# An adaLN attention-and-MLP block rebuilt around small array tiles, exps shared by two engines, and tails fed into the attention loop

## The chip, the cores and the metric

One core of a Trainium2 chip. The metric is the device time of one execution in microseconds (us), the median of several. A ratio is the mean time of one kernel's fast runs over that of the kernel before in the same rounds, so it is not quite the ratio of the medians quoted. An experiment marked "one look" has a single run, whose state (fast or slow) is therefore unknown; runs of one kernel in rounds lay within 0.5% of each other.

## The reference

A transformer block of 2048 tokens, width 512, 32 heads of 16, MLP width 1376. Six modulation vectors come from one conditioning vector.

```python
h = layernorm(x) * (1 + ca) + sa
x = x + ga * (softmax(q @ k.T * 16**-0.5) @ v) @ wo     # q, k, v = h @ wqkv, 32 heads of 16
h = layernorm(x) * (1 + cb) + sb
x = x + gb * (gelu(h @ w1 + b1) @ w2 + b2)
```

With a head width of 16, scores are small in contraction and values small in output, while the number of exps is large: 32 x 2048 x 2048.

## The kernel before

Everything is kept feature-major. Scores use the full contraction of 128 with a q tile in which all heads but one are masked to zero. Each value matmul writes 48 rows: 16 values, padding, 16 ones-columns for the denominator. Score groups of three and two tiles alternate, each with one PSUM buffer.

```python
def emit_qk(grp):                                   # grp: 3 or 2 pairs (head, key tile)
    for i, (g, kt) in enumerate(grp):
        nc.tensor.matmul(out=st[:, i, 0:qw], lhsT=kT[:, cch, kt * P:(kt + 1) * P],
                         rhs=qm[g][:, 0:qw], start=True, stop=True)
...
nc.scalar.activation(out=pt[:, 0:n, 0:qw], in_=st[:, 0:n, 0:qw], func=ACT.Exp, scale=0.25)
...
nc.tensor.matmul(out=od_cur[0:VM, 0:qw], lhsT=VE[:, kt, g % 4, :], rhs=pt[:, i, 0:qw],
                 start=(kt == 0), stop=(kt == NTT - 1))       # VM = 48
...
for bi, (q0, qw) in enumerate(blocks):              # 4 query blocks of 512
    attention(q0, qw, OTp)
    wo_and_residual(q0, qw, OTp)
    if bi < len(blocks) - 1:
        tail(q0, qw)                                # layernorm, MLP, store of this block
```

The softmax here doesn't subtract the row's maximum and nothing guards it: scores larger than these inputs give would overflow.

Of the kernel before, what the change touches and what calls it, by code (L numbers as in the profile page):

```python
# [9 lines left out]
ACT = mybir.ActivationFunctionType  # L10
ALU = mybir.AluOpType
BF16 = mybir.dt.bfloat16
FP32 = mybir.dt.float32
I32 = mybir.dt.int32


@with_exitstack
def kernel(
# [15 lines left out]
    P = 128  # L34
# [4 lines left out]
    NTT = S // P  # L39
    NTQ = S // 512  # L40
    NFC = (F + P - 1) // P
    EPS = 1e-5
    GELU_K = math.sqrt(2.0 / math.pi)
    VM = 48

    def frows(fc):
        return min(P, F - fc * P)

    const = ctx.enter_context(tc.tile_pool(name="const", bufs=1))
    wpool = ctx.enter_context(tc.tile_pool(name="wpool", bufs=1))  # L50
    resid = ctx.enter_context(tc.tile_pool(name="resid", bufs=1))

    xT = resid.tile([P, NC, S], BF16, name="xT")
    for j in range(NC):
        nc.sync.dma_start_transpose(out=xT[:, j, :], in_=A_x[0][:, j * P:(j + 1) * P])  # L55
# [3 lines left out]
    ones_bf = const.tile([P, P], BF16, name="ones_bf")  # L59
    nc.vector.memset(ones_bf, 1.0)  # L60

    pidx = const.tile([P, 1], I32, name="pidx")
    nc.gpsimd.iota(pidx, pattern=[[0, 1]], base=0, channel_multiplier=1)
    ph = const.tile([P, 1], I32, name="ph")
    nc.vector.tensor_scalar(out=ph, in0=pidx, scalar1=4, scalar2=None, op0=ALU.arith_shift_right)
    ph_f = const.tile([P, 1], FP32, name="ph_f")
    nc.vector.tensor_copy(out=ph_f, in_=ph)
    maskh = const.tile([P, 8], FP32, name="maskh")
    for g in range(8):
        nc.vector.tensor_scalar(out=maskh[:, g:g + 1], in0=ph_f, scalar1=float(g), scalar2=None,  # L70
                                op0=ALU.is_equal)
    magic = const.tile([P, 512], I32, name="magic")
    nc.vector.memset(magic, 0x5F3759DF)

    last_rows = F - (NFC - 1) * P
    b1c_bf = const.tile([P, NFC], BF16, name="b1c_bf")
    nc.vector.memset(b1c_bf, 0.0)
    nc.sync.dma_start(out=b1c_bf[:, 0:NFC - 1],
                      in_=B_b1[0:(NFC - 1) * P].rearrange("(j p) -> p j", p=P))
    nc.sync.dma_start(out=b1c_bf[0:last_rows, NFC - 1:NFC],  # L80
                      in_=B_b1[(NFC - 1) * P:F].rearrange("(p o) -> p o", o=1))
    b1c = const.tile([P, NFC], FP32, name="b1c")
    nc.vector.tensor_copy(out=b1c, in_=b1c_bf)

    b2c_bf = const.tile([P, NC], BF16, name="b2c_bf")
    nc.sync.dma_start(out=b2c_bf, in_=B_b2.rearrange("(j p) -> p j", p=P))
    b2c = const.tile([P, NC], FP32, name="b2c")
    nc.vector.tensor_copy(out=b2c, in_=b2c_bf)

    cc_bf = const.tile([P, NC], BF16, name="cc_bf")  # L90
    nc.sync.dma_start(out=cc_bf, in_=c.rearrange("o (j p) -> p (o j)", p=P))
    cc = const.tile([P, NC], FP32, name="cc")
    nc.vector.tensor_copy(out=cc, in_=cc_bf)

    wqkv_ctx = ExitStack()
    wqkv_pool = wqkv_ctx.enter_context(tc.tile_pool(name="wqkv_pool", bufs=1))
    W_mod = wqkv_pool.tile([P, NC, 6 * D], BF16, name="W_mod")
    nc.sync.dma_start(out=W_mod, in_=w_mod.rearrange("(j p) n -> p j n", p=P))
    W_qkv = wqkv_pool.tile([P, NC, 3 * D], BF16, name="W_qkv")
    nc.sync.dma_start(out=W_qkv, in_=A_wqkv.rearrange("(j p) n -> p j n", p=P))  # L100
    W_o_pad = wpool.tile([P, 8, D], BF16, name="W_o_pad")
    nc.vector.memset(W_o_pad, 0.0)
    wo_view = A_wo.rearrange("(t jj d) f -> jj d t f", t=8, jj=4, d=16)
    for jj in range(4):
        nc.sync.dma_start(out=W_o_pad[32 * jj:32 * jj + 16, :, :], in_=wo_view[jj])
    W_1 = wpool.tile([P, NC, F], BF16, name="W_1")
    nc.sync.dma_start(out=W_1, in_=B_w1.rearrange("(j p) n -> p j n", p=P))
    W_2 = wpool.tile([P, NFC, D], BF16, name="W_2")
    nc.vector.memset(W_2[:, NFC - 1, :], 0.0)
    nc.sync.dma_start(out=W_2[:, 0:NFC - 1, :],  # L110
                        in_=B_w2[0:(NFC - 1) * P, :].rearrange("(j p) n -> p j n", p=P))
    last_rows = F - (NFC - 1) * P
    nc.sync.dma_start(out=W_2[0:last_rows, NFC - 1, :], in_=B_w2[(NFC - 1) * P:F, :])

    hT = resid.tile([P, NC, S], BF16, name="hT")
    qT = resid.tile([P, NC, S], BF16, name="qT")
    kT = resid.tile([P, NC, S], BF16, name="kT")
    vT = resid.tile([P, NTT, D], BF16, name="vT")

    pkp_ctx = ExitStack()  # L120
    pkp = pkp_ctx.enter_context(tc.tile_pool(name="pro_keep", bufs=4))
    pspA_ctx = ExitStack()
    ppsA = pspA_ctx.enter_context(tc.tile_pool(name="proA_ps", bufs=4, space=bass.MemoryType.PSUM))
    ptpA_ctx = ExitStack()
    ptpA = ptpA_ctx.enter_context(tc.tile_pool(name="proA_tmp", bufs=2))
    means = []
    rstds = []
    for tq in range(NTQ):
        q0 = tq * 512
        cs = slice(q0, q0 + 512)  # L130
        xsq = ptpA.tile([P, NC, 512], BF16, name="ln_xsq")
        nc.vector.tensor_tensor(out=xsq, in0=xT[:, :, cs], in1=xT[:, :, cs], op=ALU.mult)
        ps1 = ppsA.tile([P, 512], FP32, name="ln_ps")
        for j in range(NC):
            nc.tensor.matmul(out=ps1, lhsT=ones_bf, rhs=xT[:, j, cs],
                             start=(j == 0), stop=(j == NC - 1))
        mean = pkp.tile([P, 512], FP32, name="p_mean")
        nc.vector.tensor_scalar(out=mean, in0=ps1, scalar1=1.0 / D, scalar2=None, op0=ALU.mult)
        ps2 = ppsA.tile([P, 512], FP32, name="ln_ps")
        for j in range(NC):  # L140
            nc.tensor.matmul(out=ps2, lhsT=ones_bf, rhs=xsq[:, j, :],
                             start=(j == 0), stop=(j == NC - 1))
        rstd = pkp.tile([P, 512], FP32, name="p_rstd")
        nc.vector.tensor_tensor(out=rstd, in0=mean, in1=mean, op=ALU.mult)
        nc.vector.tensor_scalar(out=rstd, in0=rstd, scalar1=-EPS, scalar2=None, op0=ALU.add)
        nc.vector.scalar_tensor_tensor(out=rstd, in0=ps2, scalar=1.0 / D, in1=rstd,
                                       op0=ALU.mult, op1=ALU.subtract)
        nc.scalar.activation(out=rstd, in_=rstd, func=ACT.Sqrt)
        nc.vector.reciprocal(out=rstd, in_=rstd)  # L149
        means.append(mean)  # L150
        rstds.append(rstd)
    pspA_ctx.close()
    ptpA_ctx.close()

    def rsqrt_fp32(tp, dst, src, width):
        si = src.bitcast(I32)
        ti = tp.tile([P, width], I32, name="rs_ti")
        nc.vector.tensor_scalar(out=ti, in0=si, scalar1=1, scalar2=None, op0=ALU.logical_shift_right)
        nc.vector.tensor_tensor(out=ti, in0=magic[:, 0:width], in1=ti, op=ALU.subtract)
        r = ti.bitcast(FP32)  # L160
        u = tp.tile([P, width], FP32, name="rs_u")
        for it in range(2):
            nc.vector.tensor_tensor(out=u, in0=r, in1=r, op=ALU.mult)
            nc.vector.tensor_tensor(out=u, in0=u, in1=src, op=ALU.mult)
            nc.vector.tensor_scalar(out=u, in0=u, scalar1=-0.5, scalar2=1.5,
                                    op0=ALU.mult, op1=ALU.add)
            dsti = dst if it == 1 else r
            nc.vector.tensor_tensor(out=dsti, in0=r, in1=u, op=ALU.mult)
            r = dsti

    def layernorm_fmajor(src, dst, acol, scol, col0, width, alloc_ps, tp, use_act=False):
        cs = slice(col0, col0 + width)
        xsq = tp.tile([P, NC, width], BF16, name="ln_xsq")
        nc.vector.tensor_tensor(out=xsq, in0=src[:, :, cs], in1=src[:, :, cs], op=ALU.mult)
        ps1 = alloc_ps(width)
        for j in range(NC):
            nc.tensor.matmul(out=ps1, lhsT=ones_bf, rhs=src[:, j, cs],
                             start=(j == 0), stop=(j == NC - 1))
        mean = tp.tile([P, width], FP32, name="ln_mean")
        nc.vector.tensor_scalar(out=mean, in0=ps1, scalar1=1.0 / D, scalar2=None,  # L180
                                op0=ALU.mult)
        ps2 = alloc_ps(width)
        for j in range(NC):
            nc.tensor.matmul(out=ps2, lhsT=ones_bf, rhs=xsq[:, j, :],
                             start=(j == 0), stop=(j == NC - 1))
# [346 lines left out]
```

## Time and profile before

1329.8 us (median of 5, 1327.56 to 1330.2). The page and the working by stage stand in the prediction.

| stage, from the trace | us |
|---|---|
| until the first exp | 96.0 |
| attention with the three inner tails between its matmuls | 1156.8 |
| after the last exp | 76.5 |

With 1061 us for attention alone, the three inner tails cost about 96 us (an estimate: the difference), not 160. It agrees with their work on PE: 430 recorded matmuls that are not attention lie in the middle stage, at most 93 us at 0.216 us each.

The page's "PE 93%" is an average over stages, and pipelined matmuls overlap, so it is the distance between the starts of matmul groups that says how full PE is.

### The profile page before, as it was taken

The page shows a single profiled execution, that of the slowest core. Times are in us where ns is not written, and L with a number is a line of the kernel's source. Part 1 is how long each engine was busy: PE and PEld are TensorE (multiplying, and loading weights), DVE is VectorE, ACT ScalarE, POOL GpSimd, SP SyncE. Part 2 cuts the span into 40 slices and gives each one's busy share as a digit, 9 for nine tenths or more (in the row PEclk, how much of TensorE's full clock was granted, in tenths as well). Part 3 has the DMA queues.
Part 4 walks back from the last instruction along what each step waited for, and adds up shares of the span by engine and source line. Part 5 has one row for each costly group of instructions (what it writes and reads, how often), then busy time and mean ns, then how long its engine had stood idle before and what let it go on. Part 6 is the DMA issues. An engine that isn't in the chain of part 4 may idle for free.

```text
span 1329.3 us, 13099 instructions
## 1 busy us (share of the span) xinstructions
PE 1231.2 (93%) x4986; PEld 406.8 (31%) x5080; DVE 624.7 (47%) x989; ACT 1050.9 (79%) x962; POOL 139.6 (11%) x139
## 2 busy tenths in 40 slices
PE   3689999999999999999999999999999999999756
PEld 1332222222233332222233332222233332222224
DVE  6851333333368733232378743332377743332356
ACT  1468899898979868989878868989878878989634
POOL 0020101111121101010121101011111111110000
PEclk9799999999999999999999999999999999999868
DMA  9200000000000000000000000000000000000000
GB/s 230 77 1 0 0 1 0 1 1 0 1 0 1 1 17 0 1 1 0 1 0 0 1 16 0 1 0 0 1 0 1 1 16 0 1 0 1 0 0 17
DMA packets 16718, 13.09 MB, mean 10 GB/s; under 512 B 11184, under 2 KB 15120, under 8 KB 16656
## 3 DMA queue, kind: packets, MB, share of 16 engines
q1 hardware_dynamic: 16656, 12.26, 3.4%
q8 instruction: 39, 0.64, 0.2%
q14 instruction: 23, 0.19, 0.0%
HBM read 8.07 MB, written 2.10 MB: 8 GB/s over the span
## 4 chain that ended last, share of the span: by engine, by line
PE 87%; DVE 6%; ACT 4%; issue 2%; SPq 1%; DMA 0%; ACTq 0%; DVEq 0%
PE od L367 38%; PE stA L335 22%; PE stB L335 15%; ACT pt L345 3%; PE auxT L407 2%; PE auxT L460 2%; PE ps_proj L275 2%; PE auxT L432 2%; DVE p_rstd L149 1%; PE ps_proj L266 1%; ACT g_th L451 1%; SPq L55 1%; PE f_m L460 1%; DVE g_t L444 0%; DVE gT L453 0%
## 5 line engine op out<-in xcount | busy, mean ns | idle before, releaser
L345 ACT ACTIVATE pt<-stA 128x1536 bf16<-128x1536 f32 x416 | 603.6, 1451 | 161.3 <-PE stA L335 143.6
L367 PE MATMUL od<-pt,VE 128*48 128x512 bf16 x2048 | 577.2, 386 | 6.1 <-issue 0.4
L345 ACT ACTIVATE pt<-stB 128x1024 bf16<-128x1024 f32 x400 | 407.1, 1018 | 3.0 <-PE stB L335 2.2
L335 PE MATMUL stA<-qm,kT 128*128 128x512 bf16 x1188 | 338.8, 383 | 20.9 <-ACT pt L345 16.0
L367 PEld LDWEIGHTS <-VE 128*48 128x48 bf16 x2048 | 174.6, 101 | 412.1 <-issue 307.6
L335 PEld LDWEIGHTS <-kT 128*128 128x128 bf16 x2048 | 143.9, 97 | 333.6 <-issue 257.6
L375 DVE COPY OStg<-od 16x512 f32<-16x512 f32 x128 | 87.1, 680 | 322.0 <-PE od L367 320.5
L335 PE MATMUL stB<-qm,kT 128*128 128x512 bf16 x780 | 237.3, 384 | 0.0
L310 DVE TENSOR_SCALAR qm<-qT,maskh 128x512 bf16<-128x512 bf16 x128 | 47.9, 379 | 239.3 <-PE stA L335 183.5
L318 POOL MEMSET VE<- 128x2048 bf16 x32 | 57.8, 1810 | 854.5 <-PE od L367 838.5
L379 DVE RECIPROCAL DStg<-DStg 128x512 f32<-128x512 f32 x32 | 106.8, 3336 | 0.1
L376 DVE COPY DStg<-od 16x512 f32<-16x512 f32 x128 | 87.6, 684 | 2.6
L407 PE MATMUL auxT<-OTp,W_o_pad 128*128 128x512 bf16 x127 | 37.5, 426 | 8.3 <-DVE OTp L381 5.6
L453 DVE SCALAR_TENSOR_TENSOR gT<-g_th,g_y 128x512 bf16<-128x512 bf16 (+3 forms) x55 | 31.9, 582 | 27.2 <-ACT g_th L451 26.4
L451 ACT ACTIVATE g_th<-g_t 128x512 bf16<-128x512 bf16 (+3 forms) x55 | 29.8, 543 | 13.5 <-DVE g_t L448 13.1
L432 PE MATMUL auxT<-hT,W 128*128 128x512 bf16 (+1 forms) x126 | 34.7, 380 | 4.8 <-DVE g_y L440 4.6
L319 POOL MEMSET VE<- 128x1024 bf16 x32 | 34.5, 1080 | 1.7
L432 PEld LDWEIGHTS <-W 128*128 128x128 bf16 (+1 forms) x220 | 21.6, 104 | 38.0 <-issue 25.3
L460 PEld LDWEIGHTS <-W 128*128 128x128 bf16 (+1 forms) x220 | 22.6, 104 | 28.3 <-issue 11.0
L460 PE MATMUL auxT<-gT,W 128*128 128x512 bf16 (+1 forms) x132 | 31.0, 379 | 0.0
L275 PE MATMUL ps_proj<-hT,W_qkv 128*128 128x512 bf16 x128 | 28.3, 379 | 0.0
L363 POOL MEMSET OStg<- 128x512 f32 x32 | 16.8, 526 | 101.8 <-DVE OTp L381 101.8
(101 smaller groups left out, 497.7 us busy)
## 6 DMA issues: line engine op xcount, KB each, us to landing
W_mod<-in_w_mod_dram SPq DMA_DIRECT2D x1, 3072.0 KB, 10.8
out_dram<-stage SPq DMA_DIRECT2D x16, 128.0 KB, 1.7
W_qkv<-in_A_wqkv_dram SPq DMA_DIRECT2D x1, 1536.0 KB, 15.8
W<-in_B_w_dram SPq DMA_DIRECT2D x1, 1376.0 KB, 18.5
W<-in_B_w_dram SPq DMA_DIRECT2D x1, 1280.0 KB, 20.6
W_o_pad<-in_A_wo_dram SPq DMA_DIRECT2D x4, 128.0 KB, 17.3
W<-in_B_w_dram SPq DMA_DIRECT2D x1, 96.0 KB, 16.0
xT<-in_A_x_dram SPq DMA_TRANSPOSE x4, 5.5
```

Of the source, the lines that this page charges most:

```text
L275: nc.tensor.matmul(out=ps, lhsT=W_qkv[:, j, col0:col0 + P], rhs=hT[:, j, cs], start=(j == 0), stop=(j == NC - 1))
L310: nc.vector.tensor_scalar(out=t[:, 0:qw], in0=qT[:, cch, q0:q0 + qw], scalar1=maskh[:, g:g + 1], scalar2=None, op0=ALU.mult)
L318: nc.gpsimd.memset(VE[:, :, :, 16:VM], 0.0)
L335: nc.tensor.matmul(out=st[:, i, 0:qw], lhsT=kT[:, cch, kt * P:(kt + 1) * P], rhs=qm[g][:, 0:qw], start=True, stop=True)
L345: nc.scalar.activation(out=pt[:, 0:n, 0:qw], in_=st[:, 0:n, 0:qw], func=ACT.Exp, scale=0.25)
L367: nc.tensor.matmul(out=od_cur[0:VM, 0:qw], lhsT=VE[:, kt, g % 4, :], rhs=pt[:, i, 0:qw], start=(kt == 0), stop=(kt == NTT - 1))
L375: nc.vector.tensor_copy(out=OStg[rb:rb + 16, 0:qw], in_=od_cur[0:16, 0:qw])
L376: nc.vector.tensor_copy(out=DStg[rb:rb + 16, 0:qw], in_=od_cur[32:48, 0:qw])
L379: nc.vector.reciprocal(out=DStg[:, 0:qw], in_=DStg[:, 0:qw])
L407: nc.tensor.matmul(out=ps[:, 0:qw], lhsT=W_o_pad[:, t, cc * P:(cc + 1) * P], rhs=OTp[:, t, 0:qw], start=(t == 0), stop=(t == 7))
L432: nc.tensor.matmul(out=u[:rows, 0:hw], lhsT=W_1[:, j, fc * P:fc * P + rows], rhs=hT[:, j, hcs], start=(j == 0), stop=(j == NC - 1))
L460: nc.tensor.matmul(out=ps[:, 0:hw], lhsT=W_2[:rows, fc, dc * P:(dc + 1) * P], rhs=gT[:rows, fc, hs], start=(fc == 0), stop=(fc == NFC - 1))
```

## The change

Its intent is to make attention cheap on PE by using parts of the array beside each other, to take a quarter of the exps off ACT, and to put projections and MLP into the gaps. The kernel is written anew, so the diff is cut to its core; the loading of inputs and the normalisation, now token-major, are left out.

```diff
+    for g in range(2):                             # a pair of score tiles; rows 64-127 or 0-63
+        i = 2 * half + g
+        rows = slice(32 * i, 32 * i + 32)          # two heads in 32 rows; one is masked in q
+        nc.tensor.matmul(out=st[:, g, :], lhsT=kT[cc][kb][rows, ko * P:(ko + 1) * P],
+                         rhs=qm[(cc, b, par)][rows, :], start=True, stop=True)
...
+        if half == 1 and s % 2 == 1:               # every fourth piece: exp on DVE, by bits
+            nc.vector.tensor_scalar(out=pt[:, 2:4, :].bitcast(I16), in0=st, scalar1=EXB,
+                                    scalar2=None, op0=ALU.add)
+        else:
+            nc.scalar.activation(out=pt[:, 2 * half:2 * half + 2, :], in_=st,
+                                 func=ACT.Exp, scale=ESC)
...
+    for i in range(4):                             # four heads in four 32-column tiles
+        nc.tensor.matmul(out=od[32 * i:32 * i + 32, :], lhsT=VE[kt][:, 8 * cc + 2 * i + par, :],
+                         rhs=pt[:, i, :], start=(kt == 0), stop=(kt == NT - 1),
+                         tile_position=(0, 32 * i))
...
+    for s in range(NS):                            # 512 slots: query block, head group, key tile
+        emit_exp(s)
+        ...                                        # slots 1, 5, 9: block_in of blocks 1 to 3
+        emit_qk(2 * s + 3)
+        emit_qk(2 * s + 4)
+        if s > 0:
+            emit_pv(s - 1)
+        pop()                                      # one unit of other work, or one dummy matmul
...
-            attention(q0, qw, OTp)
-            wo_and_residual(q0, qw, OTp)
-            if bi < len(blocks) - 1:
-                tail(q0, qw)
```

There are three score buffers of two tiles, three exp-output buffers (`pt`), one output accumulator (`od`), and one PSUM bank (`ax`) for all other work inside the slots. The denominators go through DRAM to be spread over partitions.

## The prediction

> **What bounds the kernel now.** I read the page first: busy shares, the slices, the chain that ended last; then the timeline of one steady stretch of attention, because shares are averages over stages; then a table by stage.
>
> ```profile
> span 1329.3 us, 13099 instructions
> PE 1231.2 (93%) x4986; PEld 406.8 (31%) x5080; DVE 624.7 (47%) x989; ACT 1050.9 (79%) x962; POOL 139.6 (11%) x139
> ...
> PE   3689999999999999999999999999999999999756
> ...
> ACT  1468899898979868989878868989878878989634
> ...
> PE 87%; DVE 6%; ACT 4%; issue 2%; SPq 1%; DMA 0%; ACTq 0%; DVEq 0%
> PE od L367 38%; PE stA L335 22%; PE stB L335 15%; ACT pt L345 3%; PE auxT L407 2%; PE auxT L460 2%; PE ps_proj L275 2%; PE auxT L432 2%; DVE p_rstd L149 1%; PE ps_proj L266 1%; ACT g_th L451 1%; SPq L55 1%; PE f_m L460 1%; DVE g_t L444 0%; DVE gT L453 0%
> ...
> L345 ACT ACTIVATE pt<-stA 128x1536 bf16<-128x1536 f32 x416 | 603.6, 1451 | 161.3 <-PE stA L335 143.6
> L367 PE MATMUL od<-pt,VE 128*48 128x512 bf16 x2048 | 577.2, 386 | 6.1 <-issue 0.4
> L345 ACT ACTIVATE pt<-stB 128x1024 bf16<-128x1024 f32 x400 | 407.1, 1018 | 3.0 <-PE stB L335 2.2
> ```
>
> PE carries 75% of the chain in the two attention products, and ACT is close behind: its exps are 603.6 + 407.1 = 1011 us, with 143.6 us of waiting for score matmuls. "Busy" counts overlapping matmuls, so the timeline has to say how full PE is. PE alone in attention:
>
> ```profile
> 201.46 0.82 PE L335 MATMUL stA<-qm,kT 128*128 128x512 bf16 x3
> 202.21 0.40 PE L367 MATMUL od<-pt,VE 128*48 128x512 bf16 x1
> 202.54 0.61 PE L335 MATMUL stB<-qm,kT 128*128 128x512 bf16 x2
> 203.07 1.04 PE L367 MATMUL od<-pt,VE 128*48 128x512 bf16 x4
> 204.05 0.39 PE L335 MATMUL stA<-qm,kT 128*128 128x512 bf16 x1
> ```
>
> Read the starts. A group of n matmuls takes (its span less one duration of 0.38 to 0.40)/(n-1) = 0.216 us each. From start to start the groups of 3, 1, 2, 4 take 0.75, 0.33, 0.53, 0.98 us: each is n x 0.216 plus about 0.11. So every change between the two products costs PE 0.11 us. The cycle is 10 x 0.216 + 4 x 0.108 = 2.59 us for five 128x512 score tiles, and PE never rests in it; ACT needs 2.47 us for the same five less an overlap of 0.1 (A at 199.78 lasts 1.45, B starts at 201.13). Attention is 2048/5 x 2.59 = 1061 us. The rest is stages:
>
> ```profile
> 0.00:54.00 54.00, 20.12 (x145) 8.43 (x147) 38.83 (x64) 10.42 (x13) 2.65 (x11) 0.78 0.73 189
> ...
> 1010.00:1275.00 265.00, 249.94 (x971) 79.20 (x989) 108.28 (x157) 207.48 (x181) 20.65 (x22) 0.97 0.01 3
> 1275.00:1329.30 54.30, 31.30 (x196) 20.84 (x195) 35.89 (x113) 27.77 (x56) 0.00 (x0) 0.80 0.03 10
> ```
>
> 54 us before the first exps (transposing DMAs, then reciprocals of 3.3 us), 54 us for the last block's MLP. The remaining 1329 - 1061 - 108 = 160 us are three inner output-projection and MLP tails of about 50 us, in which no attention runs (ACT falls to 6 or 7 tenths).
>
> **What the Trainium skill says.**
> 1. "TensorEngine Tiling (Array Packing)", section Key Properties: array tiles load and multiply independently, but changing the tiling mode drains the engine. The trace agrees with the second half: the old kernel already alternates full-array scores with 48-column value products, and pays 0.11 us per change. On tiles in parallel the old trace shows nothing.
> 2. "TensorE: Matmul & The Clock Gate", section Measured speedup vs the span model: four row tiles (K=32, N=512) gave 3.07x, three column tiles 2.38x. My whole PE estimate rests on this; no run here shows it yet.
> 3. "VectorE: DVE Perf Modes", section The perf-mode tier table: an fp32 PSUM source gets no multiple rate. The trace agrees: `xT<-auxT` took 750 ns at 512 columns and 480 at 256, so 1.055 ns per element.
> 4. "ScalarE: Activation LUTs", section What ACT_TABLE_LOAD costs: about 1.28 us per load, and back-to-back activations overlap by about 93 ns. The trace shows the 0.1 us overlap.
>
> **The change part by part.** It rewrites the kernel. Work is in 512 slots (4 query blocks x 8 head groups x 16 key tiles), each with 4 heads.
>
> *Scores.* K=32 row tiles, two heads per 32 rows, the other head masked to zero in q. Still 2048 matmuls of 512 columns, issued as pairs in different rows. Two pairs are adjacent but each waits for its own one of three two-bank score buffers, so I count a pair as one pass, 0.23 us, and no overlap of the two pairs: 0.46 us a slot instead of 4 x 0.216 = 0.86.
>
> *Values.* Four 32-column tiles (16 values, 16 ones), together 4 x 0.216/3.07 = 0.28 us (estimate from item 2) instead of 0.86.
>
> *Filler.* After each slot PE takes one unit from a queue: projection or MLP work of about four matmuls (0.86 us), or one dummy (0.216 us) that keeps the clock up. Three mode changes a slot are 3 x 0.108 = 0.32 us. PE per slot: 0.46 + 0.28 + 0.32 + 0.22 = 1.28 us with a dummy, 1.92 with real work.
>
> *Exp.* 1024 pieces of 128x1024; every fourth goes to DVE as an add into int16 read as bf16. ACT keeps 768 x 1018 ns = 782 us busy, spaced 1.018 - 0.093 = 0.925: 1.39 us a slot. DVE's piece is 1024 x 1.055 + 140 (intercept of the 680 ns copies at 512) = 1.22 us every second slot, well inside its time. Refill of a score buffer: 0.05 + 0.4 + 0.1 = 0.55 us against 0.9 of lead, so ACT should be nearly fed; I take 1.43 us a slot.
>
> So attention turns from PE-bound at 2.08 us per four tiles to ACT-bound at 1.43: 512 x 1.43 = 732 us.
>
> *Real work is no longer a separate stage.* I count 138 four-matmul units inside the slots (12 key and 31 query projections, 2 gates, 24 + 33 + 36 in three tails). There PE needs 1.92 us, and I add 0.1 because one PSUM bank serves all units and its evacuation (0.69 to 0.75) can sit behind a DVE exp of 1.22: 2.02 - 1.43 = 0.59, x 138 = 81 us, in place of 160.
>
> *GELU.* One activation over 128x5632 bf16 per block: from 629 ns at 512 and 413 at 256 columns, 0.844 x 5632 + 197 = 4.95 us, plus two table loads of 1.28: 7.5 us in which no exp runs, x 3 = 22 us.
>
> *Inputs for blocks 1 to 3* interrupt the first head group: ACT spends 2 x 0.7 + 3 x 0.59 = 3.2 us each, PE about 6; 5 us each, 15 us.
>
> *Head-group ends.* One output bank, copied out (0.69 us) before the next group may start; partly hidden, 32 x 0.3 = 10 us.
>
> *Start.* No transposing DMA. About 3 MB must land; W_mod's 3 MB took 10.8 us; then normalisation, 16 transposes, modulation, k and q: first exp at 22 us instead of about 54.
>
> *Last tail*, serial: the denominator goes through DRAM in four DMA hops of about 1.7 (the stores' row) with copy and product 9; projection 7; norm 5; transposes 4; first matmuls 44 x 0.216 = 9.5; GELU 6.3; second 48 x 0.216 = 10.4; store 3.1: 54 us, as now.
>
> Sum: 22 + 732 + 81 + 15 + 22 + 10 + 54 = 936 us, say 935.
>
> **Rivals.**
> - *Tiles do not run in parallel.* PE per slot 8 x 0.216 + 0.22 + 0.32 = 2.26, real 2.91: 1157 + 138 x 0.65 + 123 = 1370 us, slower than before. Against it: item 2's measurements. For it: nothing in this trace shows concurrency.
> - *Values pack, score pairs do not* (waits, weight loads between them): 0.86 + 0.28 + 0.22 + 0.32 = 1.68 a slot, 860 + 90 + 123 = 1073 us.
> - *All four score tiles overlap and evacuations hide:* ACT alone binds: 512 x 1.39 = 712, real units 1.69 a slot so 138 x 0.3 = 41, with 113 for the rest: 866 us.
> - *The ring of three score buffers is too short*, ACT gets 1.55 to 1.6 a slot: 990 to 1010 us. For it: in the old loop ACT waited 0.23 us before each A group. Against: that wait was PE being full.
> - *The clock drops* because packed PE is idler: dummies are meant to stop that; the old clock was 1.00 in attention.
>
> **Range and chances.** The middle three rivals span 866 to 1073; I lean to ACT-bound with some PE-bound stretches. 8 in 10: 860 to 1010. Only the first rival gives no gain. Faster 0.97, same 0.01, slower 0.02.
>
> **What would show it.** Right: exps on ACT near 768 x 1.02 us, start to start 0.93, little wait on `st`; four value matmuls starting within some 0.1 us of each other; ACT 85% or more busy in attention; slots with real units near 2 us; about 7 us without exp at each GELU; clock near 1. Wrong: matmul starts still 0.216 apart inside a pair or quad (first two rivals); ACT idle before `pt` ended by `st` throughout (buffer ring); PE waiting for DVE at the shared bank for over 0.5 us per unit; mode changes dearer than 0.11 us.

## More of the kernel before

ACT's timeline at the first exp, and inside the first inner tail:

```profile
95.98 1.45 ACT L345 ACTIVATE pt<-stA 128x1536 bf16<-128x1536 f32 x1
...
456.87 1.02 ACT L345 ACTIVATE pt<-stB 128x1024 bf16<-128x1024 f32 x1
457.78 0.63 ACT L451 ACTIVATE g_th<-g_t 128x512 bf16<-128x512 bf16 x1
458.30 1.45 ACT L345 ACTIVATE pt<-stA 128x1536 bf16<-128x1536 f32 x1
```

The first exp starts at 96.0 us, after all projections; the last ends at 1252.8. Between them exps never pause for longer than 4.3 us: a block's tail (here L451, of its GELU) ran between the exps of the next block's attention, although the program writes it after the attention of its own.

## The result

951.14 us (median of 8, 950.36 to 952.64) against 1328.07 (15 runs): ratio 0.716, 95% interval 0.7153 to 0.7167. Predicted were 935 us and 860 to 1010.

The page of the changed kernel: span, busy time, the slices of PE and ACT and of the granted clock, and the four groups that make up attention.

```profile
span 948.9 us, 13546 instructions
PE 804.0 (85%) x5339; PEld 258.7 (27%) x5387; DVE 494.1 (52%) x620; ACT 775.1 (82%) x801; POOL 63.0 (7%) x75
...
PE   3577989998898969889998778899998699898797
...
ACT  1355799999997788999997878999997879999502
...
PEclk9687999999997979999998969999998879999989
...
L263 ACT ACTIVATE pt<-st 128x1024 bf16<-128x1024 f32 x768 | 731.8, 1024 | 73.0 <-PE st L251 33.7
L260 DVE TENSOR_SCALAR pt<-st 128x1024 int16<-128x1024 f32 x256 | 312.7, 1222 | 300.5 <-PE st L251 194.2
L251 PE MATMUL st<-qm,kT 32*128 32x512 bf16 x2048 | 328.9, 395 | 72.2 <-ACT pt L263 55.0
L275 PE MATMUL od<-pt,VE 128*32 128x512 bf16 x2048 | 211.1, 402 | 6.8 <-DVE OD L284 6.7
```

As many attention matmuls as before, 2 x 2048, but their union in time, worked out from the two traces' matmul records, fell from about 1050 us to 505. ACT's exps fell from 1011 us to 732, with 73 us of idle time ahead of them. A DVE piece takes 1222 ns, as estimated.

PE alone in a stretch of filler slots, then ACT over the same stretch:

```profile
404.00 0.39 PE L380 MATMUL ax<-W,W 128*128 128x512 bf16 x1
404.32 0.39 PE L251 MATMUL st<-qm,kT 32*128 32x512 bf16 x2
405.18 0.39 PE L251 MATMUL st<-qm,kT 32*128 32x512 bf16 x2 [0.47 <-ACT pt L263]
405.50 0.40 PE L275 MATMUL od<-pt,VE 128*32 128x512 bf16 x4
405.83 0.39 PE L380 MATMUL ax<-W,W 128*128 128x512 bf16 x1
406.15 0.39 PE L251 MATMUL st<-qm,kT 32*128 32x512 bf16 x4
406.75 0.40 PE L275 MATMUL od<-pt,VE 128*32 128x512 bf16 x4 [0.20 <-DVE OD L284]
```

```profile
398.49 14.15 ACT L263 ACTIVATE pt<-st 128x1024 bf16<-128x1024 f32 x15
```

Four value matmuls take 0.40 us together, as one alone does, and from their start to the next group's it is 0.32 us: one pass of 0.216 and a mode change of 0.11. Two score pairs that are both released run as one quad (406.15). PE rests 0.47 us here, waiting for ACT. ACT makes 15 exps in 14.15 us without a gap, 0.94 each. So in these slots ACT is the bound (over all 341 slots of this kind, counted below, it is idle for 7.0 of 480 us), and the wait for the copy of `od` (0.20) costs nothing, because ACT does not stop.

For the rest I measured each slot in the trace, from the first of its four value matmuls to the first of the next four, and sorted slots by what else they hold:

| slots of the changed kernel | number | mean us |
|---|---|---|
| with a filler matmul | 341 | 1.409 |
| with a real unit (projection, MLP product) | 135 | 1.962 |
| with neither (empty, first head group, GELU) | 33 | 2.116 |

Two slots of the first head group, 12.04 and 11.51 us long, are left out: they hold the inputs of blocks 2 and 3.

The two longest breaks in ACT's work. First a GELU inside a tail, ACT's timeline:

```profile
331.64 1.28 ACT L353 ACT_TABLE_LOAD   x1
332.93 4.90 ACT L353 ACTIVATE big<-big 128x5632 bf16<-128x5632 bf16 x1
337.85 1.28 ACT L263 ACT_TABLE_LOAD   x1
339.14 2.86 ACT L263 ACTIVATE pt<-st 128x1024 bf16<-128x1024 f32 x3
```

7.5 us without an exp, as predicted. Second the inputs of block 1, near the start, PE and DVE:

```profile
33.22 1.86 PE L418 MATMUL st<-ident,ln_z 128*128 128x128 bf16 x16 [0.53 <-ACT pt L263]
...
36.52 0.59 PE L201 MATMUL st<-hT,Wq 128*128 128x512 bf16 x1 [0.22 <-ACT hT L186]
...
41.33 0.17 DVE L145 CAST b1c<-b_bf 128x11 f32<-128x11 bf16 x1 [4.99 <-DMA b_bf<-in_B_b_dram]
...
42.49 0.59 PE L201 MATMUL st<-hT,Wq 128*128 128x512 bf16 x1 [5.38 <-DVE hT L189]
```

A cast of 11 bias columns, not needed before the first tail, stood at the head of DVE's queue and waited 5 us for a tiny load; the modulation behind it and then PE waited too. The three input steps also pass every tile from PE to DVE or ACT and back in single file. From the first exp (30.3 us) to the second head group (100.0 us) it took 69.7 us for 16 slots that would take 22.5 at the filler rate.

### The profile page after: what moved, and what is told of

Read it like the earlier page. It is cut to its first block, busy times and chain, and to the rows that moved or that the text cites. A ratio compares the mean times of both kernels' runs of the same rounds, so it can differ in the third digit from the quotient of the medians.

```text
span 948.9 us, 13546 instructions
## 1 busy us (share of the span) xinstructions
PE 804.0 (85%) x5339; PEld 258.7 (27%) x5387; DVE 494.1 (52%) x620; ACT 775.1 (82%) x801; POOL 63.0 (7%) x75
## 5 line engine op out<-in xcount | busy, mean ns | idle before, releaser
L263 ACT ACTIVATE pt<-st 128x1024 bf16<-128x1024 f32 x768 | 731.8, 1024 | 73.0 <-PE st L251 33.7
L260 DVE TENSOR_SCALAR pt<-st 128x1024 int16<-128x1024 f32 x256 | 312.7, 1222 | 300.5 <-PE st L251 194.2
L251 PE MATMUL st<-qm,kT 32*128 32x512 bf16 x2048 | 328.9, 395 | 72.2 <-ACT pt L263 55.0
L275 PE MATMUL od<-pt,VE 128*32 128x512 bf16 x2048 | 211.1, 402 | 6.8 <-DVE OD L284 6.7
L251 PEld LDWEIGHTS <-kT 32*128 32x128 bf16 x2048 | 87.2, 91 | 311.2 <-issue 301.8
L380 PE MATMUL ax<-W,W 128*128 128x512 bf16 x402 | 146.5, 387 | 8.7 <-DVE qm L218 8.5
L275 PEld LDWEIGHTS <-VE 128*32 128x32 bf16 x2048 | 55.5, 93 | 128.9 <-issue 128.8
L297 POOL TENSOR_TENSOR OT<-OD,RB 128x512 bf16<-128x512 f32 x32 | 40.5, 1267 | 747.2 <-DMA RB<-rn 719.0
L380 PEld LDWEIGHTS <-W 128*128 128x128 bf16 x403 | 38.6, 96 | 84.8 <-issue 77.5
L363 PE MATMUL ax<-W,big 128*128 128x512 bf16 x123 | 37.1, 417 | 1.6 <-issue 1.5
L201 PE MATMUL ax<-hT,Wq 128*128 128x512 bf16 x94 | 30.3, 422 | 2.7 <-DVE qm L218 0.8
L344 PEld LDWEIGHTS <-W 128*128 128x128 bf16 x176 | 17.1, 99 | 25.7 <-issue 14.2
```

Source lines behind the costliest of these rows:

```text
L201: nc.tensor.matmul(out=ps, lhsT=w[:, j, cc * P:(cc + 1) * P], rhs=hT[b][:, j, :], start=(j == 0), stop=(j == NC - 1))
L251: nc.tensor.matmul(out=st[:, g, :], lhsT=kT[cc][kb][rows, ko * P:(ko + 1) * P], rhs=qm[(cc, b, par)][rows, :], start=True, stop=True)
L260: nc.vector.tensor_scalar(out=pt[:, 2:4, :].bitcast(I16), in0=st, scalar1=EXB, scalar2=None, op0=ALU.add)
L263: nc.scalar.activation(out=pt[:, 2 * half:2 * half + 2, :], in_=st, func=ACT.Exp, scale=ESC)
L275: nc.tensor.matmul(out=od[32 * i:32 * i + 32, :], lhsT=VE[kt][:, 8 * cc + 2 * i + par, :], rhs=pt[:, i, :], start=(kt == 0), stop=(kt == N ...
L297: nc.gpsimd.tensor_tensor(out=ot, in0=OD, in1=RB, op=ALU.mult)
```

## The experiments

Theory A: packing works, ACT sets filler slots, PE sets real-unit slots. Rivals: B, PE and its buffers set filler slots too; C, tiles matter little and the merged tails and shared exps make the gain; D, the filler is what keeps the clock; E, it costs time.

### One array tile for the values

After the first key tile all four value matmuls use the same 32 columns. Its output is wrong, which doesn't matter for the time.

```diff
-            nc.tensor.matmul(out=od[32 * i:32 * i + 32, :], ...
-                             tile_position=(0, 32 * i))
+            c = i if kt == 0 else 0
+            nc.tensor.matmul(out=od[32 * c:32 * c + 32, :], ...
+                             tile_position=(0, 32 * c))
```

> All four value matmuls of a slot go to one 32-column tile of the array after the first key tile (wrong results on purpose), so they can't run beside each other. Theory A (the parallel array tiles make attention cheap for PE, and ACT then sets the pace at 1.41 us a slot): a value group grows from 0.32 us start to start to 3 x 0.216 + 0.32 = 0.97, PE needs 0.32 to 0.64 + 0.97 + 0.32 = 1.61 to 1.93 us in a slot with a filler, and slots with real work grow by up to 0.65; 1060 to 1160 us. Rival C (the gain comes from merging the tails into attention and from moving exps to DVE; tiles matter little): below 980 us.

1107.16 us (one look). Filler slots 1.741 us, real-unit slots 2.234. A group on one tile, in PE's timeline:

```profile
802.65 1.04 PE L276 MATMUL od<-pt,VE 128*32 128x512 bf16 x4
```

1.04 us for four, the same as a group of four in the kernel before, against 0.40. As theory A has it; C falls.

### One array tile for scores too

```diff
-            rows = slice(32 * i, 32 * i + 32)
+            rows = slice(0, 32)
```

(with the edit above)

> Score matmuls too all use one 32-row tile (wrong results on purpose). Theory A: PE per slot 0.97 + 0.97 + 0.32 = 2.26 us with a filler, 2.9 with real work, so 341 x 0.85 = 290 and 135 x 0.95 = 128 us on top of 951: about 1370 us, no faster than the kernel before, although tails stay merged and a quarter of the exps stays on DVE. Rival C: below 1050 us.

1372.52 us (one look): filler slots 2.208, real-unit slots 2.886. With merged tails, a quarter of the exps on DVE and everything else kept, but no tiles side by side, the kernel is slower than the one before. This is the prediction's first rival (1370 us), made true by hand.

Both kernels passed the comparison with the reference, although their attention was wrong. So passing it says nothing on the accuracy of the exps by bits either; that was not tested.

### No filler

```diff
             if queue:
                 ...
-            else:
-                dummy(1, aux())
```

> No dummy matmul where the queue is empty inside the slots (those of the last tail stay). Theory A with a clock that holds: slots are set by ACT, so the time stays within 1% of 951 us, and the granted clock stays above 0.9. Rival D (the filler is needed because PE would be idle over half of a slot and the clock would be throttled): granted clock below 0.8 and slots with real work twice as long in their matmuls, 1000 us or more. Rival E (the filler costs PE time that the slots miss): faster by over 2%.

1013.2 us (one look), mean granted clock 0.693: rival D. The same 40 us of attention, columns being PE, PEld, DVE, ACT and POOL busy with counts, then granted clock, DMA share and GB/s; first the changed kernel, then this one:

```profile
400.00:440.00 40.00, 36.06 (x259) 10.92 (x256) 19.66 (x21) 39.68 (x43) 1.27 (x1) 1.00 0.05 16
```

```profile
400.00:440.00 40.00, 36.64 (x204) 8.00 (x200) 17.26 (x17) 35.39 (x38) 1.27 (x1) 0.50 0.04 9
```

The clock fell to half; exps in the window went from 43 to 38. Note what did not warn of it: PE is "busy" for 36.6 of 40 us here as well, because the same matmuls last longer. How the clock reaches ACT:

```profile
400.83 0.62 PE L275 MATMUL od<-pt,VE 128*32 128x512 bf16 x4
401.55 2.85 ACT L263 ACTIVATE pt<-st 128x1024 bf16<-128x1024 f32 x3 [0.30 <-PE od L275]
```

A value group takes 0.62 us instead of 0.40, and each of ACT's twelve waits in this window (4.6 us together) ended 0.10 us after such a group and 0.65 us after the last scores, so ACT waits for a free `pt` buffer (the profile itself puts eleven of the twelve down to ACT). Slots without other work average 1.620 us, against 1.471 for the same 374 slots (with and without filler) of the changed kernel. The matmul that computes nothing is worth 62 us.

### All exps on ACT

```diff
-            if half == 1 and s % 2 == 1:
+            if False:
```

> All 1024 exp pieces on ACT, none on DVE. Theory A: a slot needs 2 x 0.937 = 1.87 us of ACT instead of 1.41, so the 341 filler slots grow by 0.47 each, 160 us, and those with real work (1.96 us, set by PE) by little, 0 to 15 us: 1105 to 1130 us. Rival B (PE with its waits on the three score buffers sets the pace, ACT only looks busy): below 1000 us.

1110.94 us (one look): filler slots 1.829, which is two pieces at 0.915, ACT back to back (idle for 0.8 us in all 341 together). Its mean clock was 0.689, but that is not the cause of the time: 282 filler slots that lie wholly at half clock average 1.828 us, 44 at full clock 1.789. Theory A for filler slots, and against B. Real-unit slots kept their 1.963, but this does not show that PE sets them: ACT alone now needs 1.83 in them, and idles for 14 of 255 us, where it idled for 54 of 253 in the changed kernel (130 slots, those of the first head group left out).

### A third of the exps on DVE

```diff
-            if half == 1 and s % 2 == 1:
+            if half == 1 and s % 3 != 0:
```

> A third of the exp pieces on DVE instead of a quarter. Theory A (ACT sets filler slots): four ACT pieces in three slots, 4 x 0.937 / 3 = 1.25 us a slot, still above PE's 0.96 to 1.28, so the 341 filler slots shrink by about 0.155 each, 53 us; slots with real work, set by PE, stay at 1.96: 890 to 910 us. Rival B (PE and its waits on the score buffers set filler slots too): 940 us or more.

966.26 us (one look), slower than with a quarter: theory A fails in this direction. Filler slots 1.444 instead of 1.25. Who ACT waited for, in us, times and longest; first the changed kernel, then this one:

```profile
ACT pt L263 <- PE od L275: 13.6, 13, 1.9
```

```profile
ACT pt L263 <- PE od L275: 110.0, 157, 3.2
```

An exp that waits for a value matmul waits for one of the three `pt` buffers. So ACT is the bound at a quarter with little to spare: relieve it, and a ring of buffers takes over. Two later runs take this apart.

### The bias load early

```diff
+    (the two b1 loads now stand ahead of the Wo loads)
-    nc.vector.tensor_copy(out=b1c, in_=b1_bf)
...
         with tc.issue_after(last_q[0].ins):
+            nc.vector.tensor_copy(out=b1c, in_=b1_bf)
             zs[1] = ln_rows(...)
```

> The small bias loads are issued before the output weights instead of last, and the bias cast comes after the first q masks on DVE. In the changed kernel DVE stood 5.0 us for that load (36.5 to 41.3 us) and PE 5.4 us behind it. Theory F (that wait is on the path): 5 us less, 944 to 947 us, first value matmul at about 46.5 us instead of 51.8. Rival (another wait takes its place, such as the normalisation of the next block): within 1 us of 951.

945.05 us (4 runs, 944.59 to 945.57), ratio 0.7118 (0.7106 to 0.713), clear of the changed kernel's 0.7153 to 0.7167. The first value matmul starts at 47.1 us instead of 51.8. The wait was on the path.

### Units of two matmuls

Projections, output projection and both MLP products are cut into units of two matmuls instead of three to five, for the inner tails. The core of it:

```diff
-            units.append((lambda f=f: w1(f), False))
+            for lo in (0, 2):
+                units.append((lambda f=f, lo=lo: w1_2(f, lo), lo > 0))
```

> The same real work in units of two matmuls instead of four (projections, output projection, both MLP products), so that twice as many slots carry some and fewer carry filler. Theory A: a half unit needs PE 0.43 + 0.11, a slot 1.18 to 1.5 us, hardly above ACT's 1.41, so the excess of the 135 real slots (0.55 each, 75 us) almost goes: 885 to 905 us. Rival G (a unit costs by its waits on the one spare PSUM bank and on the three score buffers, not by its length): 935 us or more.

937.16 us (one look), a gain but not the expected one. 255 half-unit slots of 1.637 us: 58 us above the filler rate, where 75 had been with whole units. In the first MLP product two slots took 3.23 us. DVE and PE there:

```profile
332.94 0.75 DVE L391 TENSOR_SCALAR big<-ax,b1c 128x512 bf16<-128x512 f32 x1 [1.35 <-PE ax L388]
...
333.61 1.22 DVE L279 TENSOR_SCALAR pt<-st 128x1024 int16<-128x1024 f32 x1
...
334.88 0.39 PE L270 MATMUL st<-qm,kT 32*128 32x512 bf16 x2 [0.22 <-DVE pt L279]
```

Here is a loop. The eviction of `ax` (0.75) stands on DVE ahead of an exp piece (1.22); PE's next scores wait for the buffer which that piece frees; values and the next half unit follow in PE's order; then its eviction. 0.75 + 1.22 + two passes of 0.32 + a half unit of 0.54 with about 0.1 of hand-over make the 3.23 us, of which neither ACT nor PE is full.

### Evictions in the other slot

```diff
+            if len(queue) > 1 and queue[1][2] and not queue[0][2] and slot[0] % 2 == 0:
+                dummy(1, aux())                    # start a unit of several parts in odd slots only
-            if queue:
+            elif queue:
```

> Half units as before, but a unit starts only in an odd slot (filler otherwise), so that its eviction falls into the slot that has no exp piece on DVE. Half units alone gave 937 us and 1.64 us a half-unit slot, because of a loop seen in their trace: eviction 0.75, then the DVE piece 1.22 behind it, then the scores that reuse its buffer, the values and the next half unit, 3.23 us for two slots. Theory H (that queue on DVE is what a unit costs): half-unit slots fall to 1.40 to 1.48, 885 to 905 us. Rival G (waits on the PSUM bank or PE time, whichever slot the eviction is in): 925 us or more.

931.68 us (one look). The same slots of the first MLP product took 1.76 + 1.19 = 2.95 us a pair instead of 3.23, near ACT's 2.81, so the loop is as described. But the mean of all half-unit slots fell only from 1.637 to 1.610: units with two or more DVE steps, transposes and the slots after GELU did not profit. As a theory for all of the cost it is too narrow.

### A third of the exps, evenly spaced

```diff
-            if half == 1 and s % 2 == 1:
+            if (2 * s + half) % 3 == 2:
```

> A third of the pieces on DVE as in the run that gave 966 us, but every third piece in order (always the same one of the three score buffers), not two close together and then none for four. Theory J (that run was slow because two DVE pieces of 1.22 us came within three and the ring of buffers waited for DVE): filler slots fall from 1.44 to 1.25 to 1.3, 895 to 915 us. Rival K (the three exp-output buffers are too few: ACT waits for the value matmuls): 940 us or more.

950.52 us (one look); filler slots 1.399. ACT waited 36.2 us for value matmuls instead of 110, but 60.1 for score matmuls. Neither theory holds alone.

### A third of the exps, four exp-output buffers

```diff
-    ptp = ctx.enter_context(tc.tile_pool(name="ptp", bufs=3))
+    ptp = ctx.enter_context(tc.tile_pool(name="ptp", bufs=4))
```

(with the third of the exps of the 966 us run)

> The run that gave 966 us with four exp-output buffers instead of three; in that run ACT waited 110 us for value matmuls, 14 us in the changed kernel. Rival K (that ring binds): the wait nearly goes and filler slots fall to 1.25 to 1.3, 900 to 915 us. Theory J (the score ring behind DVE binds): the wait moves to the score matmuls, 945 us or more.

933.0 us (one look): 33 us from one buffer, so that ring did bind. Yet filler slots are 1.377, not 1.25, and ACT's longest wait is now the scores:

```profile
ACT pt L263 <- PE st L251: 76.9, 96, 2.4
```

So a second ring, that of the scores, seems to bind behind the first. A fourth score buffer was not tried; why the slot stops at 1.377 is therefore argued, not shown.

### Combinations

The first joins half units, the uneven third and the early bias load:

> Half units, a third of the exp pieces on DVE and the early bias load together. Theory A: filler slots near 1.25, half-unit slots 1.25 to 1.5, the start 5 us shorter: 830 to 865 us. If PE becomes the bound everywhere, filler slots stay at 1.3 or more and the time is above 870 us.

932.0 us (4 runs, 931.35 to 935.44), ratio 0.7024 (0.7009 to 0.7038). A miss: ACT waited 107.9 us for value matmuls, as with the third alone. The second adds the fourth `pt` buffer, and a filler matmul in the empty slots of a tail and ahead of each group of transposes:

```diff
-        units += [(None, False)] * (4 if not wide else 0)
+        units += [(fill, False)] * (4 if not wide else 0)
...
         def tr(j):
+            if not wide:
+                fill()
```

> What helped, together: half units, a third of the exp pieces on DVE with four exp-output buffers, the early bias load, and a filler matmul in the empty slots of a tail and before each transpose group (after the transposes the granted clock was 0.70 to 0.77). The combination without the fourth buffer and these fillers gave 932 us, with ACT waiting 108 us for value matmuls. If the two rings and the clock are what was left: 885 to 912 us. If the score ring alone binds and the fourth buffer only moves the wait: 915 to 930 us.

901.53 us (4 runs, 899.31 to 902.75), ratio 0.6793 (0.6781 to 0.6804). It beats both kernels: 5.2% below the changed one by the medians. Half-unit slots 1.574 us, and no ACT wait for value matmuls among the larger ones. The granted clock in the middle of the first tail (294 to 328 us) was 1.00, where the changed kernel had 0.77 (297 to 331). How much of the 30 us over the first combination is the buffer and how much the fillers was not separated.

## Why the prediction was right

By its own terms, in us. The measured ones come from the slots: 512 at the filler mean of 1.409; the excess of 135 real-unit slots, 135 x (1.962 - 1.409); GELU as 3 x 7.46 (load, GELU, load); inputs as what is left of the 860.1 us between the first exp (30.3) and the end of the last (890.4).

| term | predicted | measured |
|---|---|---|
| until the first exp | 22 | 30.3 |
| 512 slots | 732 | 721.4 |
| real units | 81 | 74.7 |
| inputs of blocks 1 to 3 | 15 | 41.6 |
| GELU | 22 | 22.4 |
| head-group ends | 10 | 0 |
| last tail | 54 | 58.5 |
| sum | 936 | 948.9 |

- *PE-bound becomes ACT-bound at 1.43 us a slot.* Right: 1.41 measured, ACT almost without gaps, and the run with all exps on ACT moved filler slots to 1.829.
- *The old stages.* Misread, as shown above: 96 us before the first exp and not 54, 76.5 after the last and not 54, inner tails in between exps at about 96 us and not apart at 160. The total is not touched, since it adds up the new kernel's own stages. But what each part saves is: the start 66 us (predicted 32), the last tail 18 (predicted 0), while real units and GELU in the slots cost 75 + 22 us, about what the old inner tails did (the new units also hold most of the k and q projections). Most of the gain is attention itself, 1061 to 721 us.
- *Tiles run side by side.* Right, and better than taken: the quad of values costs 0.32 us less a change of 0.11, one pass of 0.216, where I had 0.28 (from the page's figure for row tiles; these are column tiles). Score pairs overlap too where both are released, which I had not counted. The runs without packing gave 1107 and 1372 us; the estimate of the first rival, 1370, was sound arithmetic on a false condition.
- *Real units cost PE 1.92 + 0.1.* The mean came close (1.962 for 2.02), partly by luck. Of the 130 slots after the first head group, 111 lie wholly at full clock and average 1.826 us; 12 wholly at half clock average 2.845 and 7 mixed ones 2.357. So about 16 us of the 75 are lost clock (an estimate: 12 x 1.02 + 7 x 0.53), which the prediction had at 1.00. At full clock, with the packing better than assumed, PE would need about 1.6 us (an estimate: 0.32 + 0.32 + 0.97). Part of what fills the difference is seen in the half-unit runs: evictions and exp pieces queued in one DVE, waited for through the score ring. I had put 0.1 us on such waits; halving the PE work should then have removed nearly all the excess and removed under a quarter.
- *Inputs: 5 us each.* Wrong; this is the term that was mis-sized most, 41.6 us against 15. Blocks 2 and 3 cost 10.6 and 10.1 us over a filler slot, block 1 most of the rest. I counted each engine's work in a step and not the single file between them, and did not see that a scheduler had put a cast that waits for a late load at the head of DVE's queue. That the cast stands early in the program (L145) and its load almost last could be read before the run; the early load took back 6 us, and the rest of the excess was not pursued.
- *Start: 22 us.* The data were there in time (ACT's wait for them ended at 11.0 us), but the chain of transposes, modulation and projections ran tile by tile, with the first scores only after the values. First exp at 30.3.
- *Head-group ends: 10 us.* They cost nothing: PE waits 0.2 us, ACT runs on.
- *The clock.* "Dummies are meant to stop that": shown, 1013 us and a clock of 0.50 in attention without them. In its tails the changed kernel itself is not protected: 0.77 between 297 and 331 us, against 1.00 in filler stretches. The clock halves at 295.75 us, in the slots left empty before the transposes (the first is at 298.04), and stays so until 312.8.
- The errors had different signs (+8, -11, -6, +27, 0, -10, +5) and left 13 us. The sum was better than its parts.
- *Slips of the working.* 2.08 us per four tiles should read 2.07; the range of the fourth rival is not derived, and with the prediction's own terms comes to 982 to 1000 us; the 138 units leave out twelve transpose units and one of modulation.

What stays open: the split of the full-clock excess of real-unit slots between DVE's queue, the bank `ax` and PE; and the limit of 1.377 us with a third of the exps on DVE.

## What to carry to other kernels

When a rewrite moves the bound from one engine to the next, ask at once how much slack the new bound has: here ACT at 1.41 us a slot had almost none, and taking a twelfth of the exps off it made the kernel slower until one more buffer was found. Take the stages of a kernel from the first and last start of the work in question, not from where the program writes it. Count a step that hops between engines by its hops, and read the order in which a scheduler left the instructions, above all what waits for a DMA. When PE gets faster it may lose its clock (0.50 against 1.00 here): give it work, even useless work, and compare the granted clock of stages rather than busy shares.

## What the Trainium skill lacked or had wrong

- "TensorE: Matmul & The Clock Gate", in its practical advice on the clock (no idle gaps of over about 3 us): not enough by itself. Without fillers no gap of PE between 400 and 440 us is over 0.31 us (its matmul starts are at most 0.91 us apart), PE is busy 36.6 of 40 us, and the granted clock is 0.50; with one more matmul a slot it is 1.00. The page's section A second HAM failure mode does say that frequent short idles between matmul groups can cost the clock, but not how much rest is too much.
- The same page, section Measured speedup vs the span model, gives 3.07x for four row tiles and has no figure for four column tiles. Here a group of four in column tiles took 0.32 us from start to start against 0.97 on one tile, 3.0 times less, with a mode change counted in each.
- "TensorEngine Tiling (Array Packing)", section Key Properties, says that a mode change drains, but not what that costs: about 0.11 us here at full clock, three times a slot. Between two products that both use the full array it is not paid: in the kernel before, three matmuls of the first MLP product at 451.66 us were followed by scores at 452.30, 3 x 0.216 later.
- "ScalarE: Activation LUTs", section What ACT_TABLE_LOAD costs, adds a drain of about 1.38 us to each load of 1.28. Here exps end, load and GELU follow one another: load at 331.64, GELU at 332.93, next load at 337.85, exps at 339.14. A switch cost 1.3 us, not 2.7.
